# Two token blocks of a SwiGLU taken together: gate and up by a two-by-two form with 7 products for 8

## The chip, the cores and the metric

The kernel runs on one core of one Trainium2 chip. The core's engines are TensorE (PE, matrix products, with weight loads that overlap them), VectorE (DVE), ScalarE (ACT), GpSimd (POOL) and SyncE (SP, which here only issues transfers). The metric is device time in microseconds (us). Before the change it was 987.3 us, the median of three runs (985.7, 987.3 and 987.37).

## What is computed

The input is one sequence of 2048 tokens of width 640. A first stage normalises it, convolves it along the sequence with a kernel made from S4D parameters, and adds the result to the input. The second stage, which the change is about, is a feed-forward network (FFN) of inner width 1728 on the normalised rows:

```python
h = _layernorm(x, axis=-1) * (1 + cb) + sb
gate = jnp.einsum("bsd,df->bsf", h, w1)      # 640 -> 1728
up = jnp.einsum("bsd,df->bsf", h, w3)        # 640 -> 1728
out = jnp.einsum("bsf,fd->bsd", _silu(gate) * up, w2)   # 1728 -> 640
x = x + gb * out
```

`cb`, `sb` and `gb` are rows of 640 numbers that come from the conditioning input. Everything is float32.

## The kernel before

**Products.** A float32 product is made of three passes of TensorE. Each operand is split into a part that TensorE's fast float32 form holds exactly (`wh`, `xh`, `ah`: made on ACT by a copy) and the rest (`wl`, `xl`, `al`: made on DVE by a subtraction); the passes are high by high, high by rest and rest by high. A matmul here is always one 128x128 stationary operand and 512 columns.

**Tiles.** The FFN takes the tokens in four blocks of 512 (`b` = 0 to 3) and the inner width in 14 tiles `m` in the order 0, 13, 1 to 12. Tiles 0 to 12 are 128 wide. Tile 13 is 64 wide, and its gate and up lie side by side in one 128-wide operand. For each block and tile:

- `weights_load` (L704) fetches the tile's columns of w1 and w3 (two transfers of 320 KB into `wr`, L713) and its rows of w2 (320 KB into `w2r`, L718), each into a ring of two buffers, and splits them: ACT makes `wh` (L732) and `w2h` (L733), DVE makes `wl` (L741) and `w2l` (L745). For the last block DVE first multiplies `w2r` by `gb` (L730), so that the last output needs no such product.
- `up` (L800 to L802) makes gate and up, 5 slices of 128 of the width 640 by 3 passes by 2, 30 matmuls, into two of three PSUM banks `gu`.
- `gate` makes tanh on ACT (L813), two products on DVE (L814, L815), then the split of the result `a` into `ah` (ACT, L666) and `al` (DVE, L667).
- `down` (L837) adds the tile's share of the output to five PSUM banks `acc`, 15 matmuls (10 for tile 13).

`down` of a tile comes after `up` of the next tile. Where one block ends and the next begins, the `acc` banks of the old block are read by `output` (L839: DVE multiplies by `gb`, L849, and adds to `x`, L850 and L855; SP stores `x` by four transfers, L860). The new block's first `down` writes the same banks; between it and the old block's last `down` lie the 15 up matmuls of the short tile 13, which is second in the order.

**The next block's rows.** `ln2` (L669) runs once per block behind index 8 of the tile loop of the block before. It normalises 512 rows (`xn`, L680 and L682), transposes them on TensorE through the `gu` banks (`tp`, L691: 20 transposes, 4 to a bank), multiplies and adds the conditioning on DVE (`v`, L696), and splits the result into `xh` (ACT) and `xl` (DVE, L667).

**What sets the order.** The convolution stage is ordered by a planner of its own, which the change doesn't touch. In the FFN a tile scheduler orders the instructions of each engine by its own model of their times when the program is built; each engine then runs its list in that order, and a semaphore holds an instruction until its operands are there and its destination is free. An instruction that waits holds all that stands behind it on its engine. SP issues the transfers in the same way, in order.

Of the kernel before, what the change touches and what calls it, by code (L numbers as in the profile page):

```python
# [18 lines left out]
P = 128  # L19
# [263 lines left out]
class K:  # L283
# [351 lines left out]
    def inverse_load(self, name, pool, tag, bufs, j0, nj, d0, d1, other=None):  # L635

        zv = self.zd.rearrange("f r t d -> (f r) t d")
        z = [pool.tile([P, nj, d1 - d0], F32, name=f"{name}{pr}", tag=f"{tag}{pr}", bufs=bufs) for pr in range(2)]
# [21 lines left out]
    def inverse_unit(self, u, pool, ps, tag, bufs):  # L660
        z = self.inverse_load(f"iz{u}", pool, "iz", 2, 2 * u, 2, 0, D)
        self.inverse(2 * u, 2, z, ps, tag, bufs, 0, D)
# [6 lines left out]
    def ln2(self, b, pool, ps, stats=None, po=None):  # L669
# [3 lines left out]
        st, mv = stats or self.ln_begin(pool, f"n{b}")  # L673
        for j in range(4):
            self.ln_part(st, xs, j, KT - 1 if stats else 0, KT)
        rstd, nb = self.ln_end(pool, st, mv, f"n{b}")
# [6 lines left out]
        xh = pool.tile([P, KT, 512], F32R, name=f"xh{b}", tag="xh", bufs=2)  # L683
        xl = pool.tile([P, KT, 512], F32R, name=f"xl{b}", tag="xl", bufs=2)
        for k in range(KT):
# [6 lines left out]
            v = pool.tile([P, 512], F32, name=f"v{b}{k}", tag="v", bufs=3)  # L692
# [5 lines left out]
        return xh, xl  # L698

# [3 lines left out]
    def weights_load(self, b, m, wp, ahead=False):  # L703
# [21 lines left out]
        def high():  # L725
            wh = wp.tile([P, 2, KT, P], F32R, name=f"wh{b}_{m}", tag="wh", bufs=2)[:, :n]
            w2h = wp.tile([P, D], F32R, name=f"w2h{b}_{m}", tag="w2h", bufs=2)
            if b == 3:

                nc.vector.tensor_mul(w2r[:, :512], w2r[:, :512], self.gb)  # L730
# [24 lines left out]
    def ffn(self, nxt, wp, pool, ps, po, mid):  # L755

        pend = None
        for b in range(4):
            acc = None
            for i in range(14):  # L760
# [10 lines left out]
                end = (b, i) == (3, 13)  # L771
                if pend is not None:
                    self.down(*pend, *([(4, 0, 1, 2)] if end else []))
                    if i == 0:
                        self.output(b - 1, pend[1], pool, ps)
                if acc is None:
                    acc = [po.tile([P, 512], F32, name=f"acc{b}{k}", tag=f"acc{k}") for k in range(KT)]
                ah, al = self.gate(b, m, gu, pool)
                prev = pend
                pend = (m, acc, ah, al, w2h, w2l)  # L780
                mid(b, i)
# [3 lines left out]
        pt = self.turn_last(3, acc, pool, ps)  # L785
# [3 lines left out]
        self.output(3, acc, pool, ps, pt)  # L789
        self.nc = real  # L790

# [13 lines left out]
    def gate(self, b, m, gu, pool):  # L805

        nc = self.nc
        th = pool.tile([P, 512], F32, name=f"th{b}_{m}", tag="th", bufs=2)
        a = pool.tile([P, 512], F32, name=f"a{b}_{m}", tag="a", bufs=2)
        ah = pool.tile([P, 512], F32R, name=f"ah{b}_{m}", tag="ah", bufs=2)  # L810
        if m < 13:
            al = pool.tile([P, 512], F32R, name=f"al{b}_{m}", tag="al", bufs=2)
# [52 lines left out]
    def run(self):  # L865
# [106 lines left out]
        def mid(b, m):  # L972
# [4 lines left out]
            if b == 0 and m == 9:  # L977
                self.gb_row(pool, ps)
# [591 lines left out]
```

## Time and profile before

The profile is of one execution, of 987.09 us, with a span (first to last instruction) of 985.3 us. The FFN's matmuls begin at 396.49 us of the span.

| | before |
|---|---|
| time, median of 3 runs | 987.3 us |
| profiled execution, its span | 987.09 us, 985.3 us |
| PE busy | 884.0 us (90%) |
| DVE, ACT, POOL busy | 665.6 us (68%), 496.6 us (50%), 287.9 us (29%) |
| transposes of a block's output, second and third block (`to`, L1517) | from 705.18 us and 846.21 us |
| end of the last matmul group | 978.67 us |

In the views "busy" is the time in which an engine worked; x30 counts instructions; a tile's name with its buffer number left out stands for all tiles of that kind. A row of the chain of waits has its start, its length, and what the chain went through. A row of the groups has busy time and the mean length of one instruction in ns. Matmuls overlap, so a matmul that is shown with 390 ns can follow the one ahead of it after a shorter time; the distance of starts is what counts for a row of them.

### The profile page before, as it was taken

The page shows a single profiled execution, that of the slowest core. Times are in us where ns is not written, and L with a number is a line of the kernel's source. Part 1 is how long each engine was busy: PE and PEld are TensorE (multiplying, and loading weights), DVE is VectorE, ACT ScalarE, POOL GpSimd, SP SyncE. Part 2 cuts the span into 40 slices and gives each one's busy share as a digit, 9 for nine tenths or more (in the row PEclk, how much of TensorE's full clock was granted, in tenths as well). Part 3 has the DMA queues.
Part 4 walks back from the last instruction along what each step waited for, and adds up shares of the span by engine and source line. Part 5 has one row for each costly group of instructions (what it writes and reads, how often), then busy time and mean ns, then how long its engine had stood idle before and what let it go on. Part 6 is the DMA issues. An engine that isn't in the chain of part 4 may idle for free.

```text
span 985.3 us, 20196 instructions
## 1 busy us (share of the span) xinstructions
PE 884.0 (90%) x8095; PEld 707.7 (72%) x8095; DVE 665.6 (68%) x1235; ACT 496.6 (50%) x829; POOL 287.9 (29%) x293
## 2 busy tenths in 40 slices
PE   1465787889999997999999999999999999999997
PEld 1133665767888873677788888888888888888885
DVE  6998999999999774677664464464644554754443
ACT  6878788879888741532243343342333333433321
POOL 0798799889899330100000000000000000000000
PEclk9885999999999999999999999999999999999999
DMA  9955453714131297997232354223353323543311
GB/s 207 271 173 200 115 140 89 176 46 118 36 94 45 62 271 217 223 234 181 58 111 76 107 150 118 80 85 103 100 154 93 108 80 93 141 120 88 104 31 53
DMA packets 141189, 122.03 MB, mean 124 GB/s; under 512 B 13480, under 2 KB 124840, under 8 KB 139688
## 3 DMA queue, kind: packets, MB, share of 16 engines
q1 hardware_dynamic: 140360, 119.84, 45.3%
q8 instruction: 63, 1.03, 0.5%
q10 hardware_dynamic: 736, 0.92, 0.3%
q14 instruction: 30, 0.25, 0.1%
HBM read 99.75 MB, written 20.97 MB: 123 GB/s over the span
## 4 chain that ended last, share of the span: by engine, by line
PE 70%; DVE 15%; ACT 4%; DMA 3%; issue 3%; SPq 2%; POOL 2%; DVEq 0%; ACTq 0%; POOLq 0%
PE acc L837 19%; PE gu L800 12%; PE gu L801 12%; PE gu L802 12%; DVE yy L157 3%; PE ps L157 3%; PE kps L157 2%; SPq L157 2%; DVE fp L157 2%; PE fz L157 2%; DVE hn L157 2%; DVE xx L157 2%; PE fk L157 2%; PE fh L157 2%; PE iy L652 1%
## 5 line engine op out<-in xcount | busy, mean ns | idle before, releaser
L800 PE MATMUL gu<-xh,wh 128*128 128x512 f32 x540 | 210.8, 392 | 0.1
L802 PE MATMUL gu<-xh,wl 128*128 128x512 f32 x540 | 210.3, 390 | 0.0
L801 PE MATMUL gu<-xl,wh 128*128 128x512 f32 x540 | 210.3, 390 | 0.0
L732 ACT ACTIVATE wh<-wr 128x640 fp32r<-128x640 f32 x105 | 71.9, 731 | 134.3 <-PE gu L801 131.0
L744 POOL MEMSET w2l<- 64x640 f32 x3 | 1.9, 630 | 444.6 <-PE acc L837 444.6
L800 PEld LDWEIGHTS gu<-xh,wh 128*128 128x128 f32 x540 | 101.7, 189 | 21.3 <-ACT xh L666 0.5
L802 PEld LDWEIGHTS gu<-xh,wl 128*128 128x128 f32 x540 | 101.4, 188 | 21.2
L801 PEld LDWEIGHTS gu<-xl,wh 128*128 128x128 f32 x540 | 101.6, 188 | 20.8
L813 ACT ACTIVATE th<-gu 128x512 f32<-128x512 f32 x52 | 31.1, 597 | 128.7 <-PE gu L802 128.5
L815 DVE TENSOR_TENSOR a<-a,gu 128x512 f32<-128x512 f32 x52 | 35.8, 688 | 85.6 <-PE gu L802 85.4
L157 POOL TENSOR_TENSOR yy<-e,e 128x512 f32<-128x512 f32 x80 | 86.2, 1093 | 16.5 <-PE kps L157 10.5
L814 DVE SCALAR_TENSOR_TENSOR a<-th,gu 128x512 f32<-128x512 f32 x52 | 35.7, 686 | 75.2 <-ACT th L813 75.1
L837 PE MATMUL acc<-w2h,ah 128*128 128x512 f32 x219 | 85.4, 390 | 0.0
L837 PE MATMUL acc<-w2l,ah 128*128 128x512 f32 x219 | 85.4, 390 | 0.0
L733 ACT ACTIVATE w2h<-w2r 128x640 fp32r<-128x640 f32 x54 | 39.9, 739 | 88.7 <-issue 52.2
L741 DVE TENSOR_TENSOR wl<-wr,wh 128x640 fp32r<-128x640 f32 x105 | 82.4, 819 | 0.0
L157 POOL TENSOR_TENSOR ph<-p,p 128x1024 int32<-128x1024 int32 x40 | 79.9, 1996 | 7.7 <-ACT tr L157 7.0
L745 DVE TENSOR_TENSOR w2l<-w2r,w2h 128x640 fp32r<-128x640 f32 (+1 forms) x54 | 44.4, 822 | 52.9 <-ACT w2h L733 52.7
L157 DVE TENSOR_TENSOR yy<-yy,tr 128x512 f32<-128x512 f32 (+1 forms) x80 | 75.5, 945 | 0.9 <-ACT tr L157 0.6
L837 PE MATMUL acc<-w2h,al 128*128 128x512 f32 x203 | 76.1, 390 | 0.0
L157 PE MATMUL kps<-yy,xx 128*32 128x64 f32 x2560 | 52.1, 237 | 24.7 <-DVE xx L157 21.6
L157 PEld LDWEIGHTS kps<-yy,xx 128*32 128x32 f32 x2560 | 45.6, 118 | 34.3 <-issue 17.2
(231 smaller groups left out, 1692.9 us busy)
## 6 DMA issues: line engine op xcount, KB each, us to landing
wr<-in_w SPq DMA_DIRECT2D x104, 320.0 KB, 3.6
w2r<-in_w SPq DMA_DIRECT2D x52, 320.0 KB, 3.0
zd<-zt SPq DMA_DIRECT2D x39, 256.0 KB, 2.8
iz<-zd SPq DMA_DIRECT2D x24, 320.0 KB, 7.0
xs<-in_x SPq DMA_DIRECT2D x16, 320.0 KB, 11.7
hs<-hb SPq DMA_DIRECT2D x20, 256.0 KB, 2.4
xb<-hs SPq DMA_DIRECT2D x20, 256.0 KB, 4.9
x<-in_x SPq DMA_DIRECT2D x16, 320.0 KB, 9.6
```

The source lines that it names most:

```text
L157: self.prev = self.k.order(f(*a, **kw), self.prev)
L732: self.nc.scalar.activation(wh[:, i], raw[:, i], AF.Copy)
L733: self.nc.scalar.activation(w2h, w2r, AF.Copy)
L741: eng.tensor_tensor(wl[:, i], raw[:, i], wh[:, i].bitcast(F32), op=ALU.subtract)
L745: eng.tensor_tensor(w2l[q], w2r[q], w2h[q].bitcast(F32), op=ALU.subtract)
L800: nc.tensor.matmul(pg, wh[:, k, :], xh[:, k, :], start=(k == 0), stop=False)
L801: nc.tensor.matmul(pg, wh[:, k, :], xl[:, k, :], start=False, stop=False)
L802: nc.tensor.matmul(pg, wl[:, k, :], xh[:, k, :], start=False, stop=(k == KT - 1))
L813: nc.scalar.activation(th, gu[0], AF.Tanh, scale=0.5)
L814: nc.vector.scalar_tensor_tensor(a, th, 1.0, gu[0], op0=ALU.add, op1=ALU.mult)
L815: nc.vector.tensor_mul(a, a, gu[1])
L837: nc.tensor.matmul(acc[k], *two(a, w), start=(m == 0 and i == 0), stop=(m == 12 and i == 2))
```

## The change

The first two blocks run as before. For blocks 2 and 3 gate and up are made together, tile by tile for all 14 tiles, and then both blocks' down projections, block 2 first.

**The two-by-two form.** For one tile of 128, let the rows be gate and up and the columns block 2 and block 3, and cut the width 640 into slices 0 and 1, slices 2 and 3, and slice 4. Over the first two pieces this is a product of two 2x2 block matrices, which a form of Strassen's kind (Winograd's) makes with 7 block products in place of 8. A block product is 2 slices by 3 passes, 6 matmuls. Slice 4 is done plainly, 4 products of 3 matmuls. So a tile takes 7 x 6 + 12 = 54 matmuls where two blocks took 60. Tile 13 is plain, 30 matmuls as before. With it go sums: four of weights (`sums`, on POOL, 256 columns each), the token side's sums (`ln_pair`, on DVE, once), and seven of results, of which two stay in PSUM as accumulation; the rest is three copies from PSUM on ACT (`copied`) and five additions on DVE (`add`) per tile.

**Buffers.** The split weights of a tile, nine pieces, lie in one pair of 2048-column tiles, `wch` and `wcl`, which has a single buffer; ACT and DVE fill it in parts of 640, 1024 and 384 columns (`part`). The products `a` of both blocks, 13 tiles each, are kept unsplit in SBUF at the places that the list `space` names, and are split again in `pair_down`, in four slots of the same pair of tiles (`slots`). Tile 13's are kept split.

**What moves.** Block 2's `ln2` comes behind index 4 of block 1's tile loop, block 3's rows, now with the token sums in six tiles `px` (`ln_pair`), behind index 7. The last `down` and the output of block 1 stand inside the first tile of `pair_up`. `output` of block 2 now stands between two `down`s. w1 and w3 are loaded and split once for both blocks, w2 for each block (`weights2`). The first stage's buffers in SBUF are laid out anew.

```diff
-    def ln2(self, b, pool, ps, stats=None, po=None):
+    def ln_norm(self, b, pool, stats=None):
...
+    def ln_pair(self, xh, xl, pool, ps):
...
+        for p in range(2):
+            b12, b22 = turned(p), turned(p + 2)
+            t1, t2 = (pool.tile([P, 512], F32, name=f"t{i}{p}", tag="v", bufs=4) for i in (1, 2))
+            V.tensor_sub(t1, b12, xh[:, p].bitcast(F32))
+            V.tensor_sub(t1, t1, xl[:, p].bitcast(F32))
+            V.tensor_sub(t2, b22, t1)
+            keep(1, p, t1)
+            keep(2, p, t2)
+            V.tensor_sub(b12, b22, b12)
+            keep(3, p, b12)
+            keep(0, p, b22)
+            V.tensor_sub(t2, xh[:, p + 2].bitcast(F32), t2)
+            V.tensor_add(t2, xl[:, p + 2].bitcast(F32), t2)
+            keep(4, p, t2)
+        keep(5, 0, turned(4))
...
     def ffn(self, nxt, wp, pool, ps, po, mid):
...
-        for b in range(4):
+        for b in range(2):
...
+    def pair_up(self, pend, x2, wp, pool, ps, po):
...
+        S1, S2, S3, S4, A11, A12, KG, A22, KU = 0, 256, 512, 768, 1024, 1280, 1536, 1664, 1920
+
+        def mul(to, w, x, start=False, stop=False):
+            n = x[0].shape[1]
+            for k in range(n):
+                o = slice(w + k * P, w + k * P + P)
+                for i, (t, y) in enumerate(((wch, x[0]), (wch, x[1]), (wcl, x[0]))):
+                    nc.tensor.matmul(to, t[:, o], y[:, k], start=start and k == i == 0, stop=stop and (k, i) == (n - 1, 2), skip_group_check=True)
...
+        def sums(m):
...
+            G.tensor_tensor(s[0], a21, a22, op=ALU.add)
+            G.tensor_tensor(s[1], s[0], a11, op=ALU.subtract)
+            G.tensor_tensor(s[2], a11, a21, op=ALU.subtract)
+            G.tensor_tensor(s[3], a12, s[1], op=ALU.subtract)
...
+        for n, m in enumerate(order):
+            after = order[n + 1] if n + 1 < len(order) else None
+            if after is not None:
+                load(after)
+            y, z2, z5 = (bank(f"p{x}_{m}") for x in (1, 2, 5))
+            a2, a3 = place(m, 2), place(m, 3)
+            mul(y, A11, b11, True, True)
+            s1 = copied(y)
+            mul(z2, A12, b21, True)
+            mul(z2, KG, k2, stop=True)
+            add(s1, z2, s1)
+            gated(a2, s1)
+            mul(y, S2, t2, stop=True)
+            s2 = copied(y)
+            mul(z5, S1, t1, True, True)
+            add(s2, z5, s2)
+            if after is not None:
+                sums(after)
+            if n == 0:
+                self.down(*pend)
+                self.output(1, pend[1], ps)
+            z3, z4 = (bank(f"p{x}_{m}") for x in (3, 4))
+            mul(z3, S4, b22, True)
+            mul(z3, KG, k3, stop=True)
+            if after is not None:
+                whole(after, 0)
+            add(s2, z3, s2)
+            gated(a3, s2)
+            mul(y, S3, t3, stop=True)
+            s3 = copied(y)
+            if after is not None:
+                part(0, ws)
+            mul(z4, A22, t4, True)
+            mul(z4, KU, k2, stop=True)
+            c = keep.tile([P, 512], F32, name="c21", tag="oc", bufs=1)
+            add(c, z4, s3)
+            V.tensor_mul(a2, a2, c)
+            mul(z5, KU, k3, stop=True)
+            add(s3, z5, s3)
+            V.tensor_mul(a3, a3, s3)
+            if after is not None:
+                whole(after, 1)
...
+    def pair_down(self, wp, pool, ps, po):
+
+        order = (0, 1, 2, 3, 13) + tuple(range(4, 13))
+        pend = n = None
+        for b in (2, 3):
+            acc = None
+            for m in order:
+                w2h, w2l = self.weights2(b, m, wp)
...
+                    n = 0 if n is None else n + 1
+                    t = self.slots[n % 4]
+                    ah, al = t[:, :512], t[:, 512:]
+                    self.split(ah, al, self.a.pop((m, b)), self.nc.vector)
...
+                if pend is not None:
+                    self.down(*pend, *([(4, 0, 1, 2)] if end else []))
+                    if acc is None and b == 3:
+                        self.output(2, pend[1], ps)
...
+    def weights2(self, b, m, wp):
...
+        if b == 3:
+            nc.vector.tensor_mul(w2r[:, :512], w2r[:, :512], self.gb)
+        nc.scalar.activation(w2h, w2r, AF.Copy)
...
+        nc.vector.tensor_tensor(w2l[q], w2r[q], w2h[q].bitcast(F32), op=ALU.subtract)
...
-            if m == 8 and b < 3:
+            if (b, m) in ((0, 8), (1, 4)):
                 nxt[b + 1] = self.ln2(b + 1, pool, ps)
-
-        self.ffn(nxt, wp, pool, ps, po, mid)
...
+            if (b, m) == (1, 7):
+                self.ln_pair(*nxt[2], pool, ps)
+
+        pend = self.ffn(nxt, wp, pool, ps, po, between)
+        close("conv")
+        pool = open_("pair", "right")
+        self.pair_up(pend, nxt[2], wp, pool, ps, po)
+        self.pair_down(wp, pool, ps, po)
```

`V`, `A`, `G` are DVE, ACT and POOL. The changed program's lines have other numbers: DVE's `wl` is L783, `w2l` L787 (L1034 in `weights2`), the split's rest L668, the conditioned rows L723 in `ln_pair`, the product with `gb` of the last block's w2 L1029, `down` L1082, and `og`, `x` and `to` of `output` L1094, L1095 and L1100.

**How the rows move, first place: the transposed rows on DVE.** Names: `v` is a transposed slice with its conditioning, `tp` its PSUM bank, `xl` the rest of a split, `t` a token sum, `x_0` to `x_5` the six tiles of `ln_pair`. DVE before, at block 2's `ln2`:

```order
L696 TENSOR_SCALAR v_7223<-tp_7218,cols 128x512
L745 TENSOR_TENSOR w2l_8_7274<-w2r_8_7266,w2h_8_7269 128x640
L696 TENSOR_SCALAR v_7232<-tp_7227,cols 128x512
L696 TENSOR_SCALAR v_7241<-tp_7236,cols 128x512
L667 TENSOR_TENSOR xl_7217<-v_7223,xh_7216 128x512
L667 TENSOR_TENSOR xl_7217<-v_7232,xh_7216 128x512
L667 TENSOR_TENSOR xl_7217<-v_7241,xh_7216 128x512
L696 TENSOR_SCALAR v_7250<-tp_7245,cols 128x512
```

DVE after, at `ln_pair`:

```order
L723 TENSOR_SCALAR v_7245<-tp_7240,cols 128x512
L787 TENSOR_TENSOR w2l_7_7324<-w2r_7_7316,w2h_7_7319 128x640
L723 TENSOR_SCALAR v_7252<-tp_7247,cols 128x512
L732 TENSOR_TENSOR t_7254<-v_7245,xh_6931 128x512
L733 TENSOR_TENSOR t_7254<-t_7254,xl_6932 128x512
L737 TENSOR_TENSOR v_7245<-v_7252,v_7245 128x512
L668 TENSOR_TENSOR x_0_6611<-v_7252,x_0_6611 128x512
L734 TENSOR_TENSOR t_7255<-v_7252,t_7254 128x512
L668 TENSOR_TENSOR x_1_6612<-t_7254,x_1_6612 128x512
L787 TENSOR_TENSOR w2l_8_7395<-w2r_8_7387,w2h_8_7390 128x640
L723 TENSOR_SCALAR v_7277<-tp_7272,cols 128x512
```

Before, the first three `v`, each of which frees a `gu` bank, stand with one `w2l` between them. Now seven sums and rests and a second `w2l` stand between the second `v` and the third. On PE the next gate matmuls take the bank that the third `v` frees.

**Second place: PE where block 3's down projection follows block 2's** (before: where block 3 follows block 2). `acc` is an output bank, `to` the transposes of the output's last 128 columns, `oc` their input. PE before:

```order
L837 MATMUL acc_7707<-w2h_12_8653,ah_12_8711 128x512
L837 MATMUL acc_7707<-w2l_12_8658,ah_12_8711 128x512
L837 MATMUL acc_7707<-w2h_12_8653,al_12_8712 128x512
L1517 MATMUL to_8783<-ident,oc_8781 128x128 x4
L800 MATMUL gu_130_8835<-xh_8316,wh_13_8825 128x512
L801 MATMUL gu_130_8835<-xl_8317,wh_13_8825 128x512
L802 MATMUL gu_130_8835<-xh_8316,wl_13_8830 128x512
```

PE after:

```order
L1082 MATMUL acc_9071<-w2h_12_9348,wch 128x512
L1779 MATMUL to_9395<-ident,oc_9393 128x128 x4
L1082 MATMUL acc_9421<-wcl,w2h_0_9371 128x512
L1082 MATMUL acc_9421<-wcl,w2l_0_9372 128x512
L1082 MATMUL acc_9421<-wcl,w2h_0_9371 128x512
L1082 MATMUL acc_9417<-w2h_0_9371,wcl 128x512
L1082 MATMUL acc_9417<-w2l_0_9372,wcl 128x512
L1082 MATMUL acc_9417<-w2h_0_9371,wcl 128x512
L1082 MATMUL acc_9418<-w2h_0_9371,wcl 128x512
L1082 MATMUL acc_9418<-w2l_0_9372,wcl 128x512
L1082 MATMUL acc_9418<-w2h_0_9371,wcl 128x512
L1082 MATMUL acc_9421<-wch,w2h_1_9424 128x512
```

Before, the fifteen up matmuls of the short tile 13 (the last three rows are the first of them) stand between the transposes and the new block's first `acc` matmul. Now the new block's `acc` matmuls stand directly behind the transposes.

**Third place: DVE at the same change of blocks.** `og` is a quarter of the output times `gb`, read from an `acc` bank. DVE before:

```order
L849 TENSOR_TENSOR og_8788<-acc_7704,gb 128x512
L849 TENSOR_TENSOR og_8791<-acc_7705,gb 128x512
L667 TENSOR_TENSOR al_0_8813<-a_0_8811,ah_0_8812 128x512
L850 TENSOR_TENSOR x_5221<-og_8788,x_5221 128x512
L850 TENSOR_TENSOR x_5221<-og_8791,x_5221 128x512
L855 TENSOR_TENSOR x_5221<-to_8783,x_5221 128x4x128
L745 TENSOR_TENSOR w2l_13_8831<-w2r_13_8822,w2h_13_8826 64x640
L849 TENSOR_TENSOR og_8795<-acc_7706,gb 128x512
L849 TENSOR_TENSOR og_8798<-acc_7707,gb 128x512
L850 TENSOR_TENSOR x_5221<-og_8795,x_5221 128x512
```

DVE after:

```order
L1034 TENSOR_TENSOR w2l_12_9349<-w2r_12_9346,w2h_12_9348 128x640
L668 TENSOR_TENSOR wcl<-a_8000,wcl 128x512
L1034 TENSOR_TENSOR w2l_0_9372<-w2r_0_9369,w2h_0_9371 128x640
L1029 TENSOR_TENSOR w2r_1_9422<-w2r_1_9422,gb 128x512
L1094 TENSOR_TENSOR og_9400<-acc_9068,gb 128x512
L1094 TENSOR_TENSOR og_9403<-acc_9069,gb 128x512
L1095 TENSOR_TENSOR x_5218<-og_9400,x_5218 128x512
L1100 TENSOR_TENSOR x_5218<-to_9395,x_5218 128x4x128
L668 TENSOR_TENSOR wch<-awh_7749,wch 128x512
L1095 TENSOR_TENSOR x_5218<-og_9403,x_5218 128x512
L1029 TENSOR_TENSOR w2r_2_9446<-w2r_2_9446,gb 128x512
L1034 TENSOR_TENSOR w2l_1_9425<-w2r_1_9422,w2h_1_9424 128x640
```

Before, no product of `w2r` by `gb` stands among these rows. Now `og_9400` and `og_9403` stand directly behind that of the new block's second tile (`w2r_1`), and the rest `w2l_1` of the same tile stands behind the first half of the output's additions and a further product, of `w2r_2`.

233 lines of the change are left out of this document (187 added, 46 removed).

## The prediction

> **What bounds the kernel now.** I read the FFN in four views. First the busy time by windows of 50 us (per engine: busy us, instructions; then TensorE's granted clock, the DMA share and GB/s):
>
> ```profile
> core 0: us, PE busy (x) PEld busy (x) DVE busy (x) ACT busy (x) POOL busy (x), PEclk, DMA share, GB/s
> 600.00:650.00 50.00, 50.00 (x233) 41.63 (x232) 25.24 (x37) 18.88 (x29) 0.00 (x0) 1.00 0.35 100
> 750.00:800.00 50.00, 50.00 (x232) 41.66 (x231) 26.83 (x39) 17.89 (x28) 0.00 (x0) 1.00 0.32 93
> 850.00:900.00 50.00, 50.00 (x222) 41.46 (x221) 27.32 (x40) 18.31 (x29) 0.00 (x0) 1.00 0.48 132
> 900.00:950.00 50.00, 50.00 (x222) 41.42 (x221) 23.53 (x34) 15.96 (x25) 0.00 (x0) 1.00 0.30 86
> ```
>
> PE fills every window at full clock; DVE is half used, ACT a third, POOL idle. Second, PE's waits from 450 to 985 us: the answer is its head and no row, so PE waits for nothing. Third, the chain of waits from 600 us on:
>
> ```profile
> by line: PE acc L837 32.2%; PE gu L800 21.2%; PE gu L801 21.2%; PE gu L802 21.2%; PE tp L691 1.1%; PE acc L157 1.1%; PE to L1517 0.2%; DVE x L157 0.2%; PE to L157 0.1%; DVEq L1557 0.1%; issue 0.0%
> ...
> 646.49 0.87 PE tp L691 x8
> ...
> 709.07 2.04 PE acc L837 x9
> ...
> 728.34 3.40 PE acc L837 x15
> 738.54 3.40 PE acc L837 x15
> ...
> 978.69 0.69 DVE x L157
> ```
>
> It is matmuls and nothing else until the last 0.7 us. A tile is 10.20 us (728.34 to 738.54) for 45 matmuls and a `down` 3.40 us for 15: **0.2267 us a matmul**, also at 709.07, where banks alternate (2.04/9). So each matmul removed here is worth its time, unless PE then waits. The views cannot say whether it will; for that I follow, in the changed order, each wait to what satisfies it, and cost it by these rows. Fourth, the rows of work on DVE, ACT and SP that PE could wait for:
>
> ```profile
> 642.19 0.81 DVE L696 TENSOR_SCALAR v<-tp,cols 128x512 f32<-128x512 f32 x1 [1.07 <-PE tp L691]
> 642.92 0.81 DVE L745 TENSOR_TENSOR w2l<-w2r,w2h 128x640 fp32r<-128x640 f32 x1
> 643.65 1.52 DVE L696 TENSOR_SCALAR v<-tp,cols 128x512 f32<-128x512 f32 x2
> 645.09 1.89 DVE L667 TENSOR_TENSOR xl<-v,xh 128x512 fp32r<-128x512 f32 x3
> ...
> 712.20 0.69 DVE L822 SCALAR_TENSOR_TENSOR u<-th,u 64x512 f32<-64x512 f32 x1
> 712.92 0.69 DVE L823 TENSOR_TENSOR a<-u,gu 64x512 f32<-64x512 f32 x1
> ...
> 728.38 0.69 DVE L815 TENSOR_TENSOR a<-a,gu 128x512 f32<-128x512 f32 x1 [2.02 <-PE gu L802]
> 728.98 1.55 DVE L741 TENSOR_TENSOR wl<-wr,wh 128x640 fp32r<-128x640 f32 x2
> 730.45 0.69 DVE L667 TENSOR_TENSOR al<-a,ah 128x512 fp32r<-128x512 f32 x1
> ```
>
> ```profile
> 728.15 1.37 ACT L732 ACTIVATE wh<-wr 128x640 fp32r<-128x640 f32 x2 [2.52 <-PE gu L801]
> 729.42 0.61 ACT L666 ACTIVATE ah<-a 128x512 fp32r<-128x512 f32 x1
> ```
>
> ```profile
> L733 ACT ACTIVATE w2h<-w2r x13: 738/740/742, 846.3 to 964.7; 128x640 fp32r<-128x640 f32 x13
> L745 DVE TENSOR_TENSOR w2l<-w2r,w2h x13: 806/826/826, 848.5 to 965.4; 128x640 fp32r<-128x640 f32 x12, 64x640 fp32r<-64x640 f32 x1
> L730 DVE TENSOR_TENSOR w2r<-w2r,gb x12: 675/692/694, 840.7 to 949.6; 128x512 f32<-128x512 f32 x12
> ...
> DMA to landing us min/median/max: 2.8/3.3/5.1
> ```
>
> From start to start, DVE takes 0.60 us for 512 columns (728.38 to 728.98), 0.735 for 640 (two in 1.47), 0.72 where an operation needs the one ahead of it (712.20 to 712.92) and 0.72 for a `v`. By the slope between 512 and 640 columns, 1024 would take 1.14 and 384 0.47 (estimates). ACT takes 0.635 for 640, 0.61 for 512; 1024 about 1.1 (estimate). The last fence is for the `w2r` tiles after 840 us: they land 3.3 us after issue, 5.1 at worst.
>
> **The change, part by part.**
>
> *Removed.* 13 tiles x (60 - 54) = 78 matmuls; `down`, the transposes and tile 13 keep theirs. 78 x 0.2267 = **-17.7 us**, if PE stays full. Removed beside PE are 13 tiles' w1 and w3 loads and splits, which no one waited for.
>
> *Block 3's rows in `ln_pair`: +2.4 us.* In the frame of the rows above, the transposes for the last two slices ended on PE at 646.49 + 0.87 = 647.36 and the gate matmuls went on. Now these take the bank that the third `v` frees. On DVE: first `v` 642.19, `w2l` 642.92, second `v` 643.65, then from 644.37 two dependent subtractions (1.44), three operations and a rest at 0.60 each (2.40), a `w2l` (0.735), and the third `v` from 648.95 to 649.75. PE waits 649.75 - 647.36 = 2.4 us. After it the next deadlines (the fourth `v`, the gate products of the next tile) keep 0.7 to 2.5 us. Bounds: 0 if the order gives DVE a lead of 2.4 us; twice it, 4.8, if the next deadline is missed too. `ln2` of block 2 is the old step at another index: 0.
>
> *The steady pair tile: 0.* PE takes 54 x 0.2267 = 12.24 us. DVE has nine operations of 512 columns and rests of 640, 1024 and 384: 9 x 0.60 + 0.735 + 1.14 + 0.47 = 7.7 us. ACT has three copies and two tanh at 0.61, and high parts of 0.64, 1.1 and 0.5: 5.3 us. POOL's nearest row is the first of these (1.093 us for 512 columns):
>
> ```profile
> L157 POOL TENSOR_TENSOR yy<-e,e 128x512 f32<-128x512 f32 x80 | 86.2, 1093 | 16.5 <-PE kps L157 10.5
> ```
>
> Four of 256 columns lie between 2.2 us (half each) and 4.4. All fit in 12.24. The narrow spot is not a sum but a loop: `wch` and `wcl` have one buffer, so the next tile's parts are written between their last read and their next use. For the 1024-column part PE's list leaves 18 matmuls at the narrowest, 4.08 us; the work is ACT 1.1 + DVE 1.14 + two handovers, about 2.4. Slack 1.7 us. For the 640-column part some 13 matmuls, 2.95 us, against 0.64 + 0.1 for the high half that is needed first. I take 0; what happens if this cover goes is a rival below.
>
> *From gate and up to `down`: +0.3 us.* The splits of w2's third tile are ready 0.5 to 0.7 us ahead of their use, by the ACT and DVE rows above in the changed order. Between 0 and 1 us; 0.3 because the margin is about one operation.
>
> *Block 2's `down`: 0.* A tile is 15 matmuls, 3.40 us; ACT 0.61 + 0.74, DVE 0.60 + 0.735. A `w2r` buffer comes round every two tiles, 6.80 us: landing 3.3 + split 1.5, so 1.3 to 2 us spare.
>
> *Block 2 to block 3: +4.9 us.* The 15 up matmuls that covered `output` are gone, and DVE's order at this place has a chain in it. Zero is the start of block 2's last `down` on PE. The rest `w2l` of the tile before it ends at about -5.0; its buffer is loaded again, +3.4 with the issue; product with `gb` 0.7; then `w2l_12`, 0.75, at -0.15; that frees the next buffer, whose load lands at 3.25; product with `gb` to 3.95; two `og`, two additions, a rest, an addition, a further `gb` product at 0.60 to 0.7, to 8.2; `w2l_1` to 8.9 or, with a handover at each wait, 9.3. PE's side: `down` to 3.40, transposes 0.44, three groups of three matmuls, three more with the high part: 6.6, and up to 0.5 later for the first `og`. So PE waits 2.3 to 2.8 us; I take 2.7. Behind it stand three smaller waits: the next `w2h`, which waits for the last read of the bank-3 group, 0.7; the next loads on SP behind the four stores, which took
>
> ```profile
> 852.49 3.37 SPq L860 DMA_DIRECT2D out<-x  x4
> ```
>
> 0.5 of it uncovered; and one `gb` product that waits for its load at the head of DVE's queue with a needed rest behind it, 1.0. Sum 4.9. Bounds: 1.5 (the loads land in 2.8 and the later three are covered) to 9 (they land in 5.1, twice in series, +3.6).
>
> *Block 3's `down` and the tail: 0.* Two tiles in 6.80 us against landing 3.3, `gb` product 0.65, high part 0.75, rest 0.75: 5.45, 0.8 us spare after handovers.
>
> Sum, against the profiled execution's own 987.09 (span 985.3 and 1.8 around it): -17.7 + 2.4 + 0.3 + 4.9 = -10.1, so 977.0; the profiled execution lies 0.2 under the median, which leaves **977 us**. Its own range, with the bounds that are likely together, is 974 to 980.
>
> **The rivals.**
>
> *All waits hidden, 969.4 us.* 987.1 - 17.7. For: DVE idles half of each window, so any lead it builds pays the 2.4. Against: both large waits hang on an order that is fixed, and DVE cannot run ahead of a load that is not there.
>
> *The `w2r` ring decides in `down`, about 983 us.* If loads take 5.1 us, two tiles of block 3 need 5.45 + 1.8 = 7.25 us against 6.80, with handovers 0.5 to 0.8 more over some 6 pairs (3 to 4.5 us), and the change of blocks 1.8 to 3.6 more: 982 to 985. For: one load did. Against: the median is 3.3 with more traffic than will be left.
>
> *The single-buffered weights decide, 985 to 994 us.* This is the slower side. The mechanism is DVE beside POOL, which the FFN has not had so far:
>
> ```profile
> 396.47 0.69 DVE L667 TENSOR_TENSOR xl<-v,xh 128x512 fp32r<-128x512 f32 x1
> 397.51 1.41 DVE L667 TENSOR_TENSOR xl<-v,xh 128x512 fp32r<-128x512 f32 x1 [0.35 <-ACT xh L666]
> ```
>
> ```profile
> 397.09 1.28 POOL L667 TENSOR_TENSOR xl<-v,xh 128x512 fp32r<-128x512 f32 x1 [28.11 <-ACT xh L666]
> ```
>
> The same operation takes 1.41 us in place of 0.69 while POOL runs. If the 1024-column rest doubles (+1.15) and stands behind two result additions (+1.2), the 1.7 us of slack is over by 0.65; with one ACT operation ahead of the high part (0.61), by 1.3. Over 13 tiles 8 to 17 us, so 985 to 994. It decides from 0.75 us a tile on, where the 10 us are eaten. Against: POOL's sums take at most 4.4 us of 12.24, and for their own order they come before that rest, not with it.
>
> [...]
>
> *The clock, 979 to 980.5 us.* After PE's idle 2.69 us at 390.46 the granted clock fell:
>
> ```profile
> 393.15 3.23 PE L691 MATMUL tp<-ident,xn 128*128 128x128 f32 x20 [2.69 <-ACT xn L682]
> ```
>
> ```profile
> 388.00:392.00 4.00, 2.46 (x6) 0.76 (x4) 3.39 (x21) 0.00 (x0) 0.00 (x0) 1.00 0.86 199
> 392.00:396.00 4.00, 2.85 (x20) 2.83 (x20) 2.45 (x5) 2.59 (x4) 0.00 (x0) 0.82 1.01 220
> 396.00:400.00 4.00, 3.89 (x14) 2.88 (x13) 3.29 (x4) 2.91 (x6) 2.39 (x2) 0.75 1.02 215
> ```
>
> That lost 4 x 0.18 + 4 x 0.25 = 1.7 us. My two waits are 2.4 and 2.7 us long; each could cost as much, 1.7 or 3.4 in all. Against: there PE had been half idle for 12 us, here it is full on both sides.
>
> [...]
>
> *The change doesn't do what it says, 987 us:* PE's list has the 78 matmuls fewer, so this is left with the unforeseen.
>
> **How the numbers follow.** Forecast 0.55; all hidden 0.12; ring 0.11; clock 0.09; single buffer 0.10 (0.08 slower than before, 0.01 no change, 0.01 faster); unforeseen 0.03 (0.01 no change, 0.02 slower). A measurement of this kernel tells about 0.2%, 2 us, from no change (its three runs lie 1.7 us apart). Faster: 0.55 + 0.12 + 0.11 + 0.09 + 0.01 = 0.88; no change 0.01 + 0.01 = 0.02; slower 0.08 + 0.02 = 0.10. The range is 970 to 984: it leaves out most of the single buffer's case and the ends of two others.
>
> **What would show it.** PE's waits, empty so far, should have a row of about 2.4 us on DVE's `v` near 645, a pair on DVE's `og` and `w2l` of 2 to 3 us where block 3's `down` begins, and near nothing in between; tiles of gate and up 12.24 us apart; granted clock 1.00. Rows of waits for `wch` or `wcl` in every pair tile would show the single buffer; waits for `w2h` or `w2l` every second tile of `down` the ring. The prediction is wrong if the pair tiles are over 12.5 us apart, or if the two named waits are absent.

## The result, and the profile after

| | before | after |
|---|---|---|
| time, median | 987.34 us (4 runs, 985.7 to 991.15) | 976.74 us (4 runs, 976.02 to 977.17) |
| ratio, 95% interval | | 0.989 [0.9866, 0.9913] |
| profiled execution, its span | 987.09 us, 985.3 us | 976.91 us, 975.1 us |
| PE busy | 884.0 us | 866.1 us |

The forecast was 977 us in a range of 970 to 984. The time fits; below, its terms are held against the trace one by one, and they fit less well than their sum.

PE's waits from 450 us on, of the kernel after (who waited for whom; us in total, times, longest), a list that was empty before:

```profile
PE gu L1045 <- DVE v L723: 2.4, 1, 2.4
PE acc L1082 <- DVE w2l L1034: 2.2, 2, 1.8
PE acc L1082 <- ACT w2h L1030: 1.3, 2, 0.8
```

The first is the wait in `ln_pair`, the others lie behind the change from block 2's `down` to block 3's. From 690 to 900 us the list is empty: the pair tiles and the way from gate and up to `down` wait for nothing. The chain of waits of the same kernel has, beside matmuls, the two places at which other engines set the time (start, length, what):

```profile
634.07 0.72 DVE v L723
634.79 0.61 DVE t L732
635.42 0.69 DVE t L733
...
639.17 0.82 DVE v L723
...
709.75 151.23 PE p L870 x666
...
912.71 2.89 DMA w2r<-in_w
915.70 0.69 DVE w2r L1029
916.42 1.29 DVE og L1094 x2
920.11 0.60 DVE w2r L1029
920.72 0.75 DVE w2l L1034
```

The first group are the token sums ahead of the third `v`, the long row the pair tiles, and the last group a load, its product with `gb`, the output's operations and the rest `w2l` of block 3's second tile.

The windows of the same kernel (busy us and instructions per engine, then the granted clock, DMA share, GB/s):

```profile
600.00:650.00 50.00, 47.56 (x220) 39.34 (x219) 36.71 (x56) 21.59 (x36) 0.00 (x0) 0.97 0.29 83
750.00:800.00 50.00, 50.00 (x222) 41.44 (x221) 36.83 (x51) 20.16 (x33) 14.56 (x16) 1.00 0.19 53
900.00:950.00 50.00, 46.57 (x202) 36.85 (x201) 30.39 (x46) 17.44 (x27) 0.63 (x1) 1.00 0.41 114
```

PE is full in the pair tiles with DVE at 74% and POOL at 29%. In 600 to 650 us the clock is 0.97: a loss that isn't a wait.

**A stretch that doesn't move.** The first stage takes a different time from run to run, in both kernels. The FFN can be compared without it, from a place that both programs reach with the same instructions: the eight transposes that end block 1's rows. Their rows in the chain of waits, before and after:

```profile
504.54 0.87 PE tp L691 x8
```

```profile
502.80 0.87 PE tp L699 x8
```

From there to the end of the span it is 985.3 - 504.5 = **480.8 us before** and 975.1 - 502.8 = **472.3 us after**. So the change's own gain in this pair of traces is 8.5 us, and 1.7 of the 10.2 us between the spans came ahead of it. I call this length the stretch; the experiments are read by it.

### The profile page after: what moved, and what is told of

Read it like the earlier page. It is cut to its first block, busy times and chain, and to the rows that moved or that the text cites. A ratio compares the mean times of both kernels' runs of the same rounds, so it can differ in the third digit from the quotient of the medians.

```text
span 975.1 us, 20168 instructions
## 1 busy us (share of the span) xinstructions
PE 866.1 (89%) x8017; PEld 691.1 (71%) x8017; DVE 721.0 (74%) x1305; ACT 514.1 (53%) x861; POOL 334.0 (34%) x345
## 4 chain that ended last, share of the span: by engine, by line
PE 55%; DMA 3%; DVE 2%; ACT 1%; issue 1%; SPq 0%; ACTq 0%; DVEq 0%
PE p L870 16%; PE acc L1082 16%; PE gu L1045 6%; PE gu L1047 6%; PE gu L1046 6%; PE iy L653 1%; DMA w2r<-in_w 1%; DMA zd<-zt 1%; PE q L870 1%; PE tp L699 1%; DVE w2l L1034 1%; PE acc L157 0%; DMA low<-zd 0%; ACT wh L774 0%; DVE w2r L1029 0%
## 5 line engine op out<-in xcount | busy, mean ns | idle before, releaser
L1045 PE MATMUL gu<-xh,wh 128*128 128x512 f32 x270 | 105.4, 394 | 3.2 <-DVE v L723 2.4
L1047 PE MATMUL gu<-xh,wl 128*128 128x512 f32 x270 | 105.7, 392 | 0.0
L1046 PE MATMUL gu<-xl,wh 128*128 128x512 f32 x270 | 105.7, 391 | 0.0
L870 PE MATMUL p<-x,wch 128*128 128x512 f32 x312 | 92.6, 390 | 0.0
L870 PEld LDWEIGHTS p<-x,wch 128*128 128x128 f32 x312 | 58.3, 188 | 12.6 <-ACT s L905 0.4
L1045 PEld LDWEIGHTS gu<-xh,wh 128*128 128x128 f32 x270 | 51.0, 189 | 14.1 <-issue 2.6
L1046 PEld LDWEIGHTS gu<-xl,wh 128*128 128x128 f32 x270 | 51.1, 189 | 10.7 <-DVE xl L668 0.2
L157 ACT ACTIVATE tr<-ph,hpi 128x512 f32<-128x512 f32 x80 | 54.6, 690 | 4.8 <-DVE xx L157 3.1
L870 PE MATMUL p<-x,wcl 128*128 128x512 f32 x156 | 57.0, 389 | 0.0
L157 DVE TENSOR_TENSOR xx<-tr,xx 128x512 f32<-128x512 f32 x80 | 54.5, 682 | 0.3 <-ACT tr L157 0.3
## 6 DMA issues: line engine op xcount, KB each, us to landing
zd<-zt SPq DMA_DIRECT2D x39, 256.0 KB, 3.4
hs<-hb SPq DMA_DIRECT2D x20, 256.0 KB, 2.4
xb<-hs SPq DMA_DIRECT2D x20, 256.0 KB, 4.7
```

Of the source, the lines that this page charges most:

```text
L157: self.prev = self.k.order(f(*a, **kw), self.prev)
L870: nc.tensor.matmul(to, t[:, o], y[:, k], start=start and k == i == 0, stop=stop and (k, i) == (n - 1, 2), skip_group_check=True)
L1045: nc.tensor.matmul(pg, wh[:, k, :], xh[:, k, :], start=(k == 0), stop=False)
L1046: nc.tensor.matmul(pg, wh[:, k, :], xl[:, k, :], start=False, stop=False)
L1047: nc.tensor.matmul(pg, wl[:, k, :], xh[:, k, :], start=False, stop=(k == KT - 1))
```

## The experiments

All edits are to the changed kernel unless said otherwise.

### The wait for the token sums: the four slices first

```diff
+        every = [turned(k) for k in (0, 2, 1, 3)]
         for p in range(2):
-            b12, b22 = turned(p), turned(p + 2)
-            t1, t2 = (pool.tile(..., name=f"t{i}{p}", tag="v", bufs=4) for i in (1, 2))
+            b12, b22 = every[2 * p:2 * p + 2]
+            t1, t2 = (self.keep.tile(..., name=f"t{i}{p}", tag="og", bufs=2) for i in (1, 2))
```

> The four transposed slices of block 3's rows are conditioned first and the token sums come after them (the two sums go to the og buffers), so that the third v stands directly behind the second on DVE. My theory: PE's wait of 2.44 us for v goes, and with it the half clock that followed (eight matmuls at 0.427 us in place of 0.227, 1.6 us), so 976.7 - 4.0 = 972.7 us. Rival A: the half clock is not tied to that wait; then 976.7 - 2.4 = 974.3 us and a fall of the clock near 640 us without a wait ahead of it. Rival B: DVE is the limit there and the sums' delay comes back at the next gate bank, 976 to 977 us with a new row of PE's waits.

Measured: 975.56 us (974.11 to 977.55), 0.9891 [0.9869, 0.9913] of the kernel before on its chip. The edit makes all four conditioned slices ahead of the token sums. By the median it gained 1.2 us, and as a ratio to the kernel before nothing (the change has 0.989). The stretch says more: 974.0 - 505.67 = 468.3 us, **4.0 less**, as expected. The wait for `v` is gone from the list, and so is the low clock: in the trace of this run PE is full and the clock 1.00, where the change's trace has 0.68 in 640 to 644 us:

```profile
636.00:640.00 4.00, 4.00 (x23) 3.32 (x21) 4.00 (x7) 0.86 (x2) 0.00 (x0) 1.00 0.61 184
640.00:644.00 4.00, 4.00 (x22) 3.39 (x20) 4.00 (x8) 2.77 (x5) 0.00 (x0) 1.00 0.05 10
```

So without the wait no half clock came in this run, and the wait did not come back at a later bank. In the profiled execution the time as a whole hid it, since its first stage was 2.9 us later (505.67 against 502.80). The other five executions have no profile; that their first stages were late too is not shown.

### The waits behind block 2: a ring of four for w2

```diff
-        w2r = wp.tile([P, D], F32, name=f"w2r{b}_{m}", tag="w2r", bufs=2)
+        self.w2_n = getattr(self, "w2_n", -1) + 1
+        if self.w2_n % 2:
+            w2r = wp.tile([P, 2, KT, P], F32, name=f"w2r{b}_{m}", tag="wr", bufs=2).rearrange("p a k f -> p a (k f)")[:, 0]
+        else:
+            w2r = wp.tile([P, D], F32, name=f"w2r{b}_{m}", tag="w2r", bufs=2)
```

> In the down projections every second w2r goes to a free buffer of the former w1/w3 ring: a ring of four in place of two, nothing else. My theory: the waits at and behind the change from block 2 to block 3 (1.94 + 0.60 + 0.99 + 0.55 us beyond the matmuls' own distance, 4.1 in all) come from two loads in series in a ring of two; they fall to about 0.9 (the next high part still waits for the last read of a bank), so 976.7 - 3.2 = 973.5 us. Rival: output's own operations on DVE, no longer covered by up matmuls, make them; then they stay over 3 us and the time is 975.7 to 976.7 us.

Measured: 977.47 us (975.97 to 979.69), 0.9909 [0.989, 0.9929]; the stretch 975.2 - 503.77 = 471.4 us, 0.9 less where 3.2 were expected. The four waits of 4.1 us came to 3.2 us, which is also what the rival had said (over 3 us). The theory, taken alone, fell. DVE at this place, in this run:

```profile
915.25 0.82 DVE L1038 TENSOR_TENSOR w2l<-w2r,w2h 128x640 fp32r<-128x640 f32 x1
916.48 0.69 DVE L1033 TENSOR_TENSOR w2r<-w2r,gb 128x512 f32<-128x512 f32 x1 [0.41 <-DMA w2r<-in_w]
917.20 1.29 DVE L1098 TENSOR_TENSOR og<-acc,gb 128x512 f32<-128x512 f32 x2
918.41 0.68 DVE L1099 TENSOR_TENSOR x<-og,x 128x512 f32<-128x512 f32 x1
919.01 0.68 DVE L1104 TENSOR_TENSOR x<-to,x 128x512 f32<-128x512 f32 x1
919.61 0.68 DVE L668 TENSOR_TENSOR wch<-awh,wch 128x512 fp32r<-128x512 f32 x1
920.21 0.68 DVE L1099 TENSOR_TENSOR x<-og,x 128x512 f32<-128x512 f32 x1
920.81 0.82 DVE L1038 TENSOR_TENSOR w2l<-w2r,w2h 128x640 fp32r<-128x640 f32 x1
```

With more buffers the order put the product by `gb` of a still later tile ahead of the first `og` (the fourth of block 3, where the change has the second), and it waits for its load again, at the head of DVE's queue. Behind it the operations of `output` run back to back up to the `w2l` that PE needs.

### The product by gb on POOL

```diff
-            nc.vector.tensor_mul(w2r[:, :512], w2r[:, :512], self.gb)
+            nc.gpsimd.tensor_mul(w2r[:, :512], w2r[:, :512], self.gb)
```

> Block 3's products of w2r by gb go from DVE to POOL; the ring of two and all else stay as in the change. The ring of four took 0.9 us where 3.2 were expected, and in its trace the first og still stood behind a product by gb that waited 0.41 us for its load at the head of DVE's queue. New theory: what makes the waits behind block 2 is the load-bound product in DVE's in-order queue, ahead of og, the additions and w2l; off DVE, og starts when its bank is ready, w2l of the second tile is ready at 6.7 us after the start of block 2's last down against 7.5 needed, and the 1.94 us wait goes. The waits beyond the matmuls' distance fall from 4.1 to 1.6 to 2.1 us (the next high part, 0.6, and the load behind the output's stores, 1.0, stay); from the eight transposes of block 1's rows to the end of the span 470.0 to 470.5 us in place of 472.3. Rival: the operations of output themselves are what is uncovered; then the wait stays over 1 us and the stretch over 471.5. Second rival: POOL's product takes 1.1 us in place of 0.7 and shares with DVE, and the loop of load, product, split gets later: new waits in every second tile of block 3, 473 us or more.

Measured: 980.85 us (977.55 to 982.12), 0.9926 [0.9903, 0.995]; the stretch 977.9 - 505.2 = 472.7 us, 0.4 more than with the product on DVE. The new theory fell too, taken alone. The `w2l` wait shrank, from 2.2 to 0.4 us, and others grew:

```profile
PE acc L1082 <- ACT w2h L1030: 1.8, 3, 1.2
PE acc L1082 <- DVE og L1094: 0.8, 1, 0.8
PE acc L1082 <- DVE w2l L1034: 0.4, 2, 0.3
```

Summed as distances of matmuls the waits are 4.1 us, as before. The `w2h` row agrees with the second rival, though not its size (473 us or more): POOL takes longer for the product (1.29 us, DVE 0.69), in a ring that has two buffers, and a DVE operation beside it is longer (1.71 us for 0.69). The first rival's sign, a stretch over 471.5 us, is there as well; the run with three edits below decides on that one.

```profile
920.51 1.29 POOL L1029 TENSOR_TENSOR w2r<-w2r,gb 128x512 f32<-128x512 f32 x1 [1.86 <-DMA w2r<-in_w]
```

```profile
920.64 1.71 DVE L668 TENSOR_TENSOR wch<-awh,wch 128x512 fp32r<-128x512 f32 x1
```

The rest of a split, 0.69 us elsewhere, took 1.71: it began 0.13 us behind POOL's product and was done 0.55 us after that had ended at 921.80, as if it had stood until then.

### Both, with the early v

First the early `v` with the ring of four:

> Both edits together (early v, ring of four). If the two causes are apart, the gains add: 976.7 - 4.0 - 3.2 = 969.5 us, within 0.2 us of what the prediction gave for all waits hidden. Rival: one gain hides the other (the clock falls elsewhere, or the loads of the larger ring collide with the output's stores): 971 to 973 us.

Measured: 973.58 us (971.8 to 974.24), 0.9866 [0.9843, 0.9889]; the stretch 969.9 - 503.3 = 466.6 us, 5.7 less than the change's. The gains of the two edits (4.0 and 0.9) add, with 0.8 us on top, about 0.5 of it in shorter waits behind block 2. 969.5 us was out of reach, since the ring was worth less than thought.

Then the product by `gb` on POOL with it:

> Three edits together: early v, products by gb on POOL, ring of four. If the causes are apart: from the transposes of block 1's rows to the end 472.3 - 4.0 (v and the clock) - 3.3 (waits behind block 2 down to 0.8) = 465.0 us, and 976.7 - 7.3 = 969.4 us. Rival: what early v and ring gave together (466.6 us) is not bettered, because output's operations are the limit.

Measured: **971.51 us (969.87 to 972.16), 0.9832 [0.9818, 0.9847]**; the stretch 970.2 - 505.4 = 464.8 us against 465.0 expected. PE's waits from 450 us on are one row:

```profile
PE acc L1087 <- ACT w2h L1035: 0.4, 1, 0.4
```

So `output`'s own operations are not the limit: 466.6 us was bettered. The waits behind block 2 had two causes of which either keeps most of them: a ring of two, and a product in DVE's queue that waits for a load. Of 4.1 us, 3.2 stay with a ring of four alone (2.7 with the early `v` beside it), 4.1 with the product on POOL alone, and 1.1 with all three (counted as the distance of matmuls beyond 0.227 us, as all such sums here). With the product on POOL and a ring of two, no run separates what the ring costs from what POOL's slower product costs (1.29 us for 0.69 on DVE); in the ring of four that product did no such harm. This version is the fastest here, 5.5 us under the change's own repeat (977.06, below) on the same chip.

### What one of the seven products is worth

```diff
             mul(z5, S1, t1, True, True)
+            mul(z5, S1, t1, True, True)
```

> One of the seven block products is made twice in each of the 13 pair tiles (the second overwrites the first with the same numbers): 6 matmuls more a tile, the PE work of the plain form, with everything else of the change kept. My theory: PE sets the time of the pair tiles and a matmul is worth 0.2267 us, so 78 x 0.2267 = 17.7 us more, 994.4 us, 7 us slower than the kernel before. Rival: part of the gain came from splitting and loading w1 and w3 once for two blocks; then the eighth product costs clearly less, 988 to 992 us. Second rival: the single-buffered weights are near their limit and longer tiles give them room; then also less than 17.7.

Measured: 993.44 us (991.96 to 995.08), 1.0071 [1.0047, 1.0094]: slower than the kernel before. The stretch is 992.1 - 502.35 = 489.8 us, **17.5 more** for 78 matmuls, 0.224 us each. PE waits for nothing in the pair tiles of this run either. So the gain is the product left out: with eight products the pairing, with its w1 and w3 loaded and split once, is 9.0 us longer in the stretch than the kernel before (489.8 against 480.8), of which the waits and the half clock are 8.1.

### DVE beside POOL: the weight sums twice

```diff
-            G.tensor_tensor(s[0], a21, a22, op=ALU.add)
...
+            for _ in range(2):
+                G.tensor_tensor(s[0], a21, a22, op=ALU.add)
...
```

> POOL makes its four weight sums of each pair tile twice (the same numbers again). It tests the rival by which DVE beside POOL uses up the slack of the single-buffered weights. POOL's 3.7 us a tile become 7.4. My theory: DVE, busy 8.8 us a tile now, loses at most 1.2 us more in proportion and stays under 12.24; no wait for wch or wcl, time within 1 us of the change's. Rival: DVE loses POOL's whole time, or the sums end too late for the 1024-column part: PE waits in every pair tile, 5 to 30 us slower.

Measured: 978.09 us (977.61 and 978.58), the stretch 976.8 - 504.4 = 472.4 us, 0.1 more than the change's. The pair tiles from 715 to 845 us, of the change and of this run:

```profile
715.00:845.00 130.00, 130.00 (x575) 107.24 (x574) 95.33 (x128) 52.29 (x84) 40.43 (x44) 1.00 0.22 61
```

```profile
715.00:845.00 130.00, 130.00 (x576) 107.63 (x575) 100.15 (x130) 53.26 (x85) 77.02 (x84) 1.00 0.24 63
```

POOL's sums became 7.3 us a tile in place of 3.7 (77.02 us for 84 instructions, eight a tile, and 40.43 for 44, four a tile). DVE's busy time rose by 4.8 us in 130, with two instructions more in the window, so by at most 0.45 us a tile. PE waited for nothing. The rival by which POOL eats the slack of the single-buffered weights is out for this load and twice this load.

### The change and the kernel before, again

> The changed kernel once more, unedited, beside the others on one chip. In the traces so far the first stage ended up to 2.9 us apart (the transposes of block 1's rows start between 502.35 and 505.67 us) without any edit there. My theory: the wait of 2.44 us for v comes again, to 0.05 us; whether a half clock follows it depends on where it falls against the clock's own windows of 3.413 us; the stretch from the transposes to the end is 472.3 us with the half clock and 470.7 without. Rival: the half clock comes in every run.

Measured: 977.06 us (975.98 to 979.88), 0.9897 [0.988, 0.9913]. The wait for `v` came again, with 2.4 us. The half clock did not. The clock's low stretch in the first trace lasted from 641.45 to 644.86 us, 3.41 us. The repeat has a low stretch of the same length at 386.30 us. Cut into lengths of that size, counted from the low stretch of each trace, the two runs read:

```profile
638.03:641.45 3.42, 1.32 (x6) 1.13 (x7) 3.42 (x6) 0.76 (x3) 0.00 (x0) 1.00 0.29 86
641.45:644.86 3.41, 3.41 (x10) 2.64 (x9) 3.41 (x7) 0.52 (x1) 0.00 (x0) 0.50 0.03 10
```

```profile
635.46:638.87 3.41, 2.13 (x14) 1.64 (x12) 3.41 (x6) 2.41 (x4) 0.00 (x0) 1.00 0.19 72
638.87:642.28 3.41, 2.25 (x10) 1.91 (x11) 3.41 (x6) 0.63 (x1) 0.00 (x0) 1.00 0.31 96
642.28:645.69 3.41, 3.41 (x17) 2.83 (x16) 3.41 (x7) 1.96 (x4) 0.00 (x0) 1.00 0.00 0
```

In the first, 2.1 us of the wait fell into one window (PE busy 1.32 us), and the next window ran at half clock. In the repeat the same wait was cut in two (2.13 and 2.25 busy), and nothing followed. The stretch was 974.2 - 502.7 = 471.5 us: 1.6 saved by the clock and 0.9 lost to a later load in block 3 (PE's wait for `w2h` 2.2 us in place of 1.3), so neither 470.7 nor 472.3.

The kernel before was profiled twice more, to see where the gain beyond the stretch came from:

> The kernel before, unedited, once more with a profile. The medians say that the change gained 10.6 us, the traces that only 8.5 to 9.3 of it lie behind the transposes of block 1's rows (480.9 us from there to the end before, 472.5 with a half clock and 471.6 without it after). My theory: the rest is the spread of the first stage, which no edit touches in its order; the transposes start between 502 and 506 us here too, and the stretch behind them is 480.9 us to 0.1. Rival: the new places of the first stage's buffers make it 1 to 2 us shorter; then the kernel before starts them at 505 to 507 us each time.

Measured, in this run: 989.25 us; the transposes at 506.68 us, the stretch 987.4 - 506.7 = 480.7.

> The same as the run ahead of it, a third profile of the kernel before: theory 502 to 506 us and 480.9 us behind it; rival 505 to 507 us.

Measured: 986.02 us; the transposes at 503.50 us, the stretch 984.2 - 503.5 = 480.7. Their rows:

```profile
506.68 0.87 PE tp L691 x8
```

```profile
503.50 0.87 PE tp L691 x8
```

The stretch repeats to 0.1 us; the first stage varies by 3 us in the kernel before (503.5, 504.5, 506.7) and by as much over the nine profiles of the changed kernel and its variants (502.4 to 505.7). So part of a difference between two profiles, or between two medians of four runs, can be this spread and not the change. The rival's sign, 505 to 507 us each time, failed. A smaller gain from the new places of the first stage's buffers is not ruled out: the three profiles of the kernel before average 504.9 us, the two of the unedited change have 502.8 and 502.7, and all nine average 504.0.

## Why the prediction was right, point by point

**The saved matmuls, -17.7 us: right.** The eighth product cost 17.5.

**The wait in `ln_pair`, +2.4 us: right in place, size and mechanism.** DVE in the kernel after, in the order that the prediction summed:

```profile
632.52 0.81 DVE L723 TENSOR_SCALAR v<-tp,cols 128x512 f32<-128x512 f32 x1 [1.08 <-PE tp L721]
633.25 0.82 DVE L787 TENSOR_TENSOR w2l<-w2r,w2h 128x640 fp32r<-128x640 f32 x1
633.98 0.81 DVE L723 TENSOR_SCALAR v<-tp,cols 128x512 f32<-128x512 f32 x1
634.70 0.68 DVE L732 TENSOR_TENSOR t<-v,xh 128x512 f32<-128x512 f32 x1
...
638.44 0.82 DVE L787 TENSOR_TENSOR w2l<-w2r,w2h 128x640 fp32r<-128x640 f32 x1
639.17 0.81 DVE L723 TENSOR_SCALAR v<-tp,cols 128x512 f32<-128x512 f32 x1
```

From the first `v` to the end of the third it is 7.46 us; the sum gave 7.56. Between the second and the third stand six sums and rests and a `w2l`, as the prediction summed, and not seven, as the section on the change has it.

**What followed it was a rival.** The half clock, given 0.09 and priced at 1.7 us a wait, came behind this wait in the profiled run: eight matmuls 0.427 us apart in place of 0.227, 1.6 us. So the sign "granted clock 1.00" failed. The reason given against this rival was weak: ahead of the wait at 390 us in the kernel before PE was not half idle but busy 9.44 us of 12 (378.4 to 390.4). Behind the wait at 919 us the half clock did not come (that window, from 917.93, had PE busy 1.80 us of 3.41).

**The pair tiles, 0: right.** 666 matmuls of the stage are one piece of the chain shown above, 151.23 us: 0.2271 us each, 12.26 us for 54. DVE's 1024-column rest came out as estimated, 1.14 us from start to start (731.42 to 732.56), and POOL's four sums at 3.7 us a tile, between the bounds. **From gate and up to `down`, +0.3: it was 0.**

**Block 2 to block 3, +4.9 us: 4.1.** Counted as the distance of matmuls beyond 0.227 us, the four waits are 1.94, 0.60, 0.99 and 0.55. The first, at its row

```profile
919.11 0.62 PE L1082 MATMUL acc<-w2h,wch 128*128 128x512 f32 x2
921.51 0.50 PE L1082 MATMUL acc<-wch,w2l 128*128 128x512 f32 x1 [1.78 <-DVE w2l L1034]
```

was sized 2.7. Of the pair that was to show it, on `og` and `w2l`, only `w2l` came. The term that was off in it is the load: 3.3 us to landing, taken from the kernel before. In the kernel after w2 landed sooner (the `w2r` tiles from 900 to 965 us); that this is because no w1 and w3 load beside it is likely, but no run tests it:

```profile
DMA to landing us min/median/max: 2.7/2.8/4.4
```

That is 0.5 us less, with two loads in series; the wait came out 0.8 shorter than sized. The three smaller waits were summed as 2.2 and came to 2.14, though each was off: 0.7 for 0.60, 0.5 (the loads behind the stores) for 0.99, 1.0 (the product at the head of DVE's queue) for 0.55. The step that named the cause was right as a chain and too narrow as a claim: the chain had two links, and cutting either one alone gained 0.9 us or nothing. With both cut, and the early `v`, 3.0 of the 4.1 went.

**The sum.** -17.7 + 2.4 + 0.3 + 4.9 = -10.1 was the forecast for the FFN. The stretch moved by -8.5: -17.5 + 2.4 + 1.6 (clock) + 4.1 = -9.4, which is 0.9 us off. Counted from start to start of all matmuls in the two traces, the 78 matmuls are -17.7, the wait for `v` 2.7, the clock 1.6 and the four waits 4.1. Another 1.0 lies in single matmuls that start up to 0.34 us apart and not 0.227, as the first ones behind each wait do. The rest is 0.3 in a slightly longer distance everywhere and a tail behind the last matmul that is 0.4 us shorter; together -8.4. What made 977 come out was the first stage, 1.7 us earlier in that execution. No edit touches its order, but its buffers lie in new places, and the runs don't show whether the 1.7 us are spread alone. The range held the time by its working; that the median hit the forecast to 0.3 us is luck of two errors with opposite signs.

**The other rivals.** All waits hidden (969.4): no, but the variant with three edits comes to 971.5 and keeps 1.1 us of waits. The ring that decides (983): it didn't in every second tile, as loads got faster and not slower; one late load in the repeat cost 0.9 us. The single buffer (985 to 994): no wait for `wch` or `wcl` in any of nine runs, not with POOL's work doubled.

## What to carry to other kernels

Where one engine is full and waits for nothing, work taken off it is worth its full time (here 17.5 us for 78 matmuls of 0.2267), and the loss is found by following each wait in the new order of the engines that feed it: an operation that waits for a load, put ahead of others in an in-order queue, and a ring without a spare buffer were here each enough to keep most of the loss, so try them together before ruling either out. Compare from a place that both programs reach alike; a first stage that varies by 3 us hides an edit worth 4.

## What the runs showed of the hardware

**The half clock depends on where a wait falls.** Six of the profiles have the wait of 2.4 us for `v`. In five (the change, the ring of four, the eighth product, the product on POOL, the sums twice) a stretch of 3.41 us at half clock followed, in one (the repeat) not. In windows of that length, counted from each trace's own low stretch, PE was busy 0.97 to 1.32 us of the window ahead of it, and 2.1 and 2.3 us of the two that the wait fell into in the repeat. Windows ahead of the FFN place the border more closely: in the repeat (first rows below) a window with 1.55 us busy is followed by a half clock, in the run with three edits (second rows) one with 1.60 us is not.

```profile
382.89:386.30 3.41, 1.55 (x12) 1.26 (x12) 0.24 (x2) 0.00 (x0) 0.00 (x0) 1.00 0.49 143
386.30:389.71 3.41, 3.41 (x9) 1.48 (x8) 3.17 (x18) 0.00 (x0) 0.00 (x0) 0.50 0.56 141
```

```profile
383.67:387.08 3.41, 1.60 (x4) 0.38 (x2) 0.00 (x0) 0.00 (x0) 0.00 (x0) 1.00 0.42 117
387.08:390.50 3.42, 3.01 (x19) 1.96 (x20) 1.70 (x9) 0.00 (x0) 0.00 (x0) 1.00 0.13 37
```

From 380 us on, all windows of the kernel before and of the change fall on these two sides: PE was busy at most 1.40 us of those ahead of a half clock (the one from 391.14 us, before) and at least 1.80 us of the others (the one from 917.93 us, after). Before 215 us, with other matmuls, they do not: in the kernel before PE was busy 1.82 us of the window from 90.77 us, itself at half clock, and the next one is at half clock too. So busy time alone is not the whole rule. The low stretches of one trace lie whole windows apart: in the change from 385.45 to 641.45 us, 256.0 us or 75 times 3.413, and in the kernel before from 210.23 to 394.55 us, 184.3 us or 54 times 3.413. A window ahead of a half clock need not be idle: in the repeat PE was busy for 45% of one (the 1.55 us above).

**POOL and DVE.** Doubling POOL's time in the pair tiles cost DVE at most 0.45 us a tile for 3.7 us of POOL's, far from all of it. A single operation can lose much more: the rest of a split, 0.69 us elsewhere, took 1.71 beside POOL's product of 1.29 us. Why the sum over a stage is small is seen in part in a pair tile of the change:

```profile
734.11 1.05 POOL L890 TENSOR_TENSOR ws<-ws,wp 128x256 f32<-128x256 f32 x1
735.24 1.07 POOL L892 TENSOR_TENSOR ws<-wp,ws 128x256 f32<-128x256 f32 x1
```

```profile
734.49 1.22 DVE L950 TENSOR_TENSOR a<-a,c 128x512 f32<-128x512 f32 x1
735.64 0.68 DVE L907 TENSOR_TENSOR s<-p,s 128x512 f32<-128x512 f32 x1
```

The product `a<-a,c`, which reads two tiles in SBUF, began inside POOL's sum and took 1.22 us, ending 0.55 us after it. The addition `s<-p,s`, which reads one of its two from PSUM, began inside POOL's next sum and took its usual 0.68. That the place of the operands makes the difference is read from these rows and was not tested by a run of its own.
